# One core, attention and two feed-forward stages: a new order by hand of the attention work, with three pairs of groups under way at first

## The chip, the cores and the metric

The kernel runs on one core of a Trainium2 chip. The metric is the time of one execution on the device, in microseconds. The kernel before took 896.36 us (median of 2 runs, 894.23 to 898.49).

## The reference, cut to what matters

```python
def _attn_ref(q, k, v):                       # 4 batches, 8 heads, 576 positions, 64 wide, float32
    scores = 1.0 / np.sqrt(D) * np.matmul(q, k.transpose(0, 1, 3, 2))
    mask = (rel >= 0) & (rel < 64)            # each position sees itself and the 63 before it
    scores = np.where(mask, scores, -1000000000.0)
    attn = np.exp(scores - np.max(scores, axis=-1, keepdims=True))
    attn = attn / (np.sum(attn, axis=-1, keepdims=True) + 1e-09)
    return np.matmul(attn, v)
# heads side by side: x is 2304 x 512
h = (x @ w1) * (x @ w2) @ w3                  # 512 -> 1024 -> 1024
x = h @ w_out                                 # 1024 -> 512
h = x @ w_in                                  # 512 -> 2048
out = np.maximum(0.01 * h, h) @ w_out2        # 2048 -> 512
```

The weights arrive as 64-bit floats, which the kernel turns into 32-bit ones with bit operations.

## The kernel before

**Two phases.** In the first, three batches of four, every engine runs in an order that is written out by hand: each instruction is tied to the one before it on its engine (class `Strict`, L62). This phase holds the attention of all four batches, the conversion of weights, and `x @ w1` times `x @ w2` of batches 0 to 2. In the second (batch 3, the product of `w3` and `w_out`, and the two layers behind it), a scheduler sets the order.

**Steps.** The order of the first phase comes from numbered steps. `slot` (L509) does one: PE's attention events of this step, then one `ab` group (12 matmuls of 288 columns for `x @ w1` or `x @ w2`, L542), then the eviction of the group of the step before, then all other events of this step by rank, the small ranks first. `plan` (L467) and the table `PAIRS` (L461) say in which step each event stands. The first `HEAD` = 15 steps have no `ab` group. Each of batches 0 to 2 has 32 steps with one.

**A pair of groups.** A group `(m, hh, gr)` is three blocks of 64 queries for two heads, `m` = 2 x batch + quad of heads, `hh` the half of the quad, `gr` = 0 to 2. A pair is both halves. If its step is t, PE does `scores` in t (24 matmuls, which the trace shows as 48) and VectorE the six `maxima`; ScalarE the exponentials (`exps`) in t + 1 and t + 2, one half in each; `normal` (L221: sum plus 1e-9 on POOL, reciprocal on VectorE, multiplication on POOL) in t + 2 and t + 3; PE turns `s` (`turn`, `mm<-ident,s`) in t + 3 and t + 4, and it is copied out (`turned`); `av` and `av_out` stand in t + 4 and t + 5. `av_out` casts the result for `x` (ScalarE) and subtracts the cast from it (VectorE), as each 32-bit operand is split in a high and a low part. `prep` (L172) transposes `q` and `k` of the next quad on VectorE, six calls for each. The `pa` accumulator is one tile, whose halves take turns.

**Conversions.** `advance` (L323) moves a pipeline of units of 512 columns on by one: ScalarE scales the unit (`f`), and for `w1` and `w2` takes its low bits (`low_bits`, L318, into one buffer `low`); VectorE shifts and joins bits, one unit behind; and `store` (L280) casts the finished unit for `w` on ScalarE, and POOL (`w1`, `w2`) or VectorE (`w_out`) computes the low part `w<-f,w`. `f` has four buffers. Loads are issued by SP when a unit's bits are done.

**Products.** `b_out` (L560) multiplies the two `ab` groups on VectorE. Every eighth step (every fourth in parts of batch 0) two sums on POOL follow, `t3` and `p32`, as part of the eviction, ahead of the step's other events. Their stores `pb<-t` and `pb<-p` are put three steps later on SP. `t3` has one buffer.

## Time and profile before

| | us |
|---|---|
| median of 2 runs | 896.36 (894.23 to 898.49) |
| the profiled execution | 894.67 |
| its span, first to last instruction | 892.5 |
| TensorE matmul (PE) busy | 814.0 (91%) |
| VectorE (DVE) busy | 606.8 (68%) |
| ScalarE (ACT) busy | 459.6 (51%) |
| GpSimd (POOL) busy | 99.4 (11%) |

The profile is of one execution. PE is TensorE's matmuls, PEld its weight loads, SP the engine that issues transfers. The granted clock is the share of full speed that TensorE was allowed. Nearly all instructions go through one helper, so their line is L78 (ordered phase) or L76 (scheduled phase) and they are told apart by the names of tiles: `mm` scores and turns, `pa` the `av` accumulator, `ab`, `pr` and `o` the accumulators of the layers. In a row, `out<-in` names what is written and read, `x48` is the number of instructions in it, and a bracket says how long the engine had been idle and what released it.

### The profile page before, as it was taken

To read this page: it belongs to the slowest core of one execution; us is meant where nothing else is said; L and a number is where in the kernel's file an instruction comes from. 1 tells how busy PE (TensorE), PEld (TensorE's weight loads), DVE (VectorE), ACT (ScalarE), POOL (GpSimd) and SP (SyncE) were. 2 spreads that over 40 slices of the span, in tenths; PEclk is the share of its full clock that TensorE was granted. 3 is DMA by queue.
4 is the path that set the end of the run, shared out by engine and by line. 5 is a ranking of instruction groups with operands and counts; after the bars stand their busy time and mean duration, and the time that the engine had idled before them with its cause. 6 is when DMAs were issued, how large, how long until landed. Compare 5 with 4: busy or idle time off the path is not lost.

```text
span 892.5 us, 18232 instructions
## 1 busy us (share of the span) xinstructions
PE 814.0 (91%) x6856; PEld 777.2 (87%) x6856; DVE 606.8 (68%) x1446; ACT 459.6 (51%) x1103; POOL 99.4 (11%) x149
## 2 busy tenths in 40 slices
PE   3566869989897899999999999999999999999998
PEld 2355759988797889889999999999999999999998
DVE  5446453566355728688577888687775999897966
ACT  2445434444254443353455656565555886666644
POOL 2234242322222221000000000000000000000000
PEclk9667889999899999999999999999999999999999
DMA  9328534467343627655267745699899864443422
GB/s 275 120 81 203 191 106 137 125 171 216 129 101 96 175 68 225 214 163 164 77 195 213 222 145 168 213 305 349 303 320 294 281 210 158 119 149 110 142 72 71
DMA packets 121544, 157.96 MB, mean 177 GB/s; under 512 B 42736, under 2 KB 82928, under 8 KB 121456
## 3 DMA queue, kind: packets, MB, share of 16 engines
q1 hardware_dynamic: 121312, 156.66, 56.8%
q8 instruction: 54, 0.88, 0.4%
q14 instruction: 34, 0.28, 0.1%
q10 hardware_dynamic: 144, 0.13, 0.0%
HBM read 104.07 MB, written 52.69 MB: 176 GB/s over the span
## 4 chain that ended last, share of the span: by engine, by line
PE 71%; DVE 9%; ACT 5%; DMA 5%; POOL 4%; issue 4%; SPq 1%; POOLq 0%; DVEq 0%; ACTq 0%
PE pr L76 29%; PE o L76 20%; PE ab L78 10%; PE mm L78 6%; DVE f L78 3%; PE ab L76 2%; PE mm L76 2%; DMA wd<-f 2%; PE pa L78 2%; DMA pb<-t 2%; POOL s L78 2%; ACT s L78 1%; DVE f L76 1%; POOL w L78 1%; DVE qT L78 1%
## 5 line engine op out<-in xcount | busy, mean ns | idle before, releaser
L78 PE MATMUL ab<-x,w 128*128 128x288 f32 x1152 | 179.1, 311 | 0.0
L78 PEld LDWEIGHTS ab<-x,w 128*128 128x128 f32 x1152 | 164.4, 199 | 5.5 <-issue 3.6
L76 PE MATMUL pr<-yop,w 128*128 128x384 f32 x900 | 161.0, 337 | 0.5 <-ACT c L76 0.5
L76 PEld LDWEIGHTS pr<-yop,w 128*128 128x128 f32 x900 | 157.5, 188 | 1.3 <-ACT c L76 1.2
L76 PE MATMUL o<-yop,yop 128*128 128x256 f32 x777 | 94.9, 282 | 0.0
L76 PEld LDWEIGHTS o<-yop,yop 128*128 128x128 f32 x777 | 93.6, 189 | 0.0
L76 ACT COPY c<-pr 128x384 f32<-128x384 f32 x95 | 45.2, 479 | 63.3 <-PE pr L76 55.5
L78 PE MATMUL mm<-ident,s 128*128 128x128 f32 x144 | 30.6, 331 | 51.1 <-POOL s L78 46.9
L76 ACT CAST yop<-raw 128x256 fp32r<-128x256 f32 (+2 forms) x116 | 54.3, 491 | 37.2 <-PE o L76 33.8
L78 PEld LDWEIGHTS mm<-ident,s 128*128 128x128 f32 x144 | 19.2, 164 | 58.2 <-POOL s L78 57.1
L76 DVE TENSOR_TENSOR yop<-raw,yop 128x256 fp32r<-128x256 f32 (+2 forms) x116 | 58.0, 524 | 16.9 <-ACT yop L76 16.5
L78 ACT ACTIVATE s<-s,nm 128x128 f32<-128x128 f32 x144 | 56.1, 393 | 17.9 <-DVE nm L78 17.8
L76 ACT CAST yop<-f 128x512 fp32r<-128x512 f32 (+2 forms) x102 | 54.9, 567 | 18.6 <-DVE f L76 15.8
L76 DVE TENSOR_TENSOR yop<-f,yop 128x512 fp32r<-128x512 f32 (+2 forms) x102 | 59.3, 617 | 3.5 <-ACT yop L76 3.5
L76 DVE TENSOR_TENSOR c<-pr,c 128x384 f32<-128x384 f32 x74 | 40.7, 552 | 27.8 <-PE pr L76 13.7
L76 PEld LDWEIGHTS ab<-x,w 128*128 128x128 f32 x384 | 53.3, 188 | 1.8
L76 PE MATMUL ab<-x,w 128*128 128x288 f32 x384 | 54.8, 295 | 0.0
L76 PE MATMUL mm<-wf,w3T 128*128 128x512 f32 x192 | 51.0, 401 | 0.4 <-ACT w3T L76 0.4
L78 DVE TENSOR_TENSOR x<-pa,x 128x192 fp32r<-128x192 f32 x48 | 17.0, 354 | 46.4 <-ACT x L78 46.2
L78 DVE TENSOR_TENSOR p<-ab,io 128x288 f32<-128x288 f32 x48 | 21.7, 453 | 38.2 <-ACT s L78 13.4
L78 ACT COPY io<-ab 128x288 f32<-128x288 f32 x48 | 19.1, 397 | 54.2 <-PE ab L78 53.2
L78 DVE CUSTOM_DVE_ANT_0 s<-mm,mask 128x128 f32<-128x128 f32 x144 | 32.3, 287 | 20.2 <-PE mm L78 20.2
(121 smaller groups left out, 1438.0 us busy)
## 6 DMA issues: line engine op xcount, KB each, us to landing
hd<-c SPq DMA_DIRECT2D x96, 192.0 KB, 4.1
raw<-hd SPq DMA_DIRECT2D x32, 512.0 KB, 3.8
raw<-in_moe_w_dram SPq DMA_DIRECT2D x28, 512.0 KB, 4.6
raw<-in_moe_w_out_dram SPq DMA_DIRECT2D x24, 512.0 KB, 5.0
pb<-p SPq DMA_DIRECT2D x32, 288.0 KB, 4.6
raw<-in_moe_w_in_dram SPq DMA_DIRECT2D x16, 512.0 KB, 4.3
wd<-f SPq DMA_DIRECT2D x32, 256.0 KB, 4.6
raw<-wd SPq DMA_DIRECT2D x30, 256.0 KB, 4.6
```

The lines of the kernel that those rows point to most:

```text
L76: return f(*a, **k)
L78: r = f(*a, **k)
```

## The change

- `HEAD` is 13, and the pairs of batch 0 stand two steps apart instead of three (`PAIRS`); the pairs of batches 1 to 3 stand one to two steps earlier against the batch's first step.
- In batch 0 the scores stand ahead of the turns of their step. In batches 1 to 3 both halves' exponentials stand in t + 1, both divisions in t + 2 (the second behind the conversions of that step, rank 6.5), both turns in t + 4.
- In all batches both `av` stand in t + 5, with a new `pa` tile for each pair; the cast of the result is `x_hi` in t + 5, the subtraction `x_lo` in t + 6.
- `low` has two buffers, in turn; `pts` has two instead of three.
- The low part `w<-f,w` of a unit stands one step behind its cast, rank 1.
- The sums `t3` and `p32` stand at the end of their step (rank 8).
- Six transposes of the second quad stand in steps 0 and 1 instead of 0 to 2; `q` and `k` of the third quad are loaded in step 3 instead of 14, into other buffers; at the end of batch 2 the last conversions stand ahead of the last events.

```diff
@@ -58,7 +58,7 @@
-    HEAD = 15
+    HEAD = 13
@@ -150,7 +150,7 @@
     def loads_qk(m):
         b, quad = divmod(m, 2)
-        raw_qk[m] = [spare_tile("wf")[:, 0:EQ * D] if b else xb.tile([P, 2, S], F32, name="x", tag="x").rearrange("p s c -> p (s c)")
+        raw_qk[m] = [spare_tile("wf")[:, 0:EQ * D] if m > 2 else xb.tile([P, 2, S], F32, name="x", tag="x").rearrange("p s c -> p (s c)")
@@ -233,7 +233,7 @@
     def turned(g):
-        pts = att.tile([P, GT, P], F32, name="pts", bufs=3)
+        pts = att.tile([P, GT, P], F32, name="pts", bufs=2)
         (act.copy if g[0] > 1 else dve.tensor_copy)(pts, grp[g])
         grp[g] = pts
 
@@ -242,11 +242,9 @@
         b, quad = divmod(m, 2)
         vt = vts[2 * m + hh]
         pts = grp[g]
-        if not pa:
-            t = ps_at.tile([P, 4, P], F32, name="pa", tag="pa").rearrange("p t k -> p (t k)")
-            pa.extend(t[:, 2 * P * i:2 * P * i + GT * W] for i in range(2))
-        pa.append(pa.pop(0))
-        o = grp[g] = pa[-1]
+        if hh == 0:
+            pa[:] = [ps_at.tile([P, 4, P], F32, name="pa", tag="pa").rearrange("p t k -> p (t k)")]
+        o = grp[g] = pa[0][:, 2 * P * hh:2 * P * hh + GT * W]
         for t in range(GT):
             l = GT * gr + t
             a, n = (0, max(l - 1, 0) // 2) if (l % 2 or l == 0) else (1, (l - 2) // 2)
@@ -255,16 +253,19 @@
                 pe.matmul(o[W * h:W * h + W, W * t:W * t + W], lhsT=vt[:, (a + h) % 2, n + h * (4 + a), :],
                           rhs=pts[:, t, W * c:W * c + W], start=True, stop=True)
 
-    def av_out(g):
+    def xcols(g):
         m, hh, gr = g
         b, hp = m // 2, 2 * (m % 2) + hh
-        o = grp.pop(g)
         if (b, hp) not in xt:
             xt[b, hp] = xtile(b)
-        x = xt[b, hp]
-        cols = slice(gr * GT * W, (gr + 1) * GT * W)
-        act.copy(x[:, 0, cols], o)
-        dve.tensor_tensor(out=x[:, 1, cols], in0=o, in1=f32(x[:, 0, cols]), op=ALU.subtract)
+        return (xt[b, hp][:, i, gr * GT * W:(gr + 1) * GT * W] for i in range(2))
+
+    def x_hi(g):
+        act.copy(next(xcols(g)), grp[g])
+
+    def x_lo(g):
+        hi, lo = xcols(g)
+        dve.tensor_tensor(out=lo, in0=grp.pop(g), in1=f32(hi), op=ALU.subtract)
 
 
     def wslot(key):
@@ -284,14 +285,20 @@
                 slots[key] = wslot(key)
             t, sl = slots[key], slice(UC * half, UC * half + UC)
             act.copy(t[:, 0, sl], f)
-            (pool if key[0] in ("w1", "w2") else dve).tensor_tensor(out=t[:, 1, sl], in0=f, in1=f32(t[:, 0, sl]),
-                                                                     op=ALU.subtract)
+            later(1, lambda: (pool if key[0] in ("w1", "w2") else dve).tensor_tensor(
+                out=t[:, 1, sl], in0=f, in1=f32(t[:, 0, sl]), op=ALU.subtract), 1)
         return fin
+
+    def later(d, f, rank=8):
+        if Strict.on:
+            at(clock["t"] + d, rank, f)
+        else:
+            f()
 
...
@@ -316,7 +323,8 @@
         return t.rearrange("p k m -> p (k m)") if len(t.shape) == 3 else t
 
     def low_bits(u):
-        u["low"] = stage.tile([P, UC], I32, name="low", tag="low", bufs=1)
+        n_of["low"] += Strict.on
+        u["low"] = (att if n_of["low"] % 2 else stage).tile([P, UC], I32, name="low", tag="low", bufs=1)
         act.activation(out=u["low"], in_=flat(u["raw"]).bitcast(U8).rearrange("p (m e) -> p m e", e=8)[:, :, 3],
                        func=AF.Copy, scale=1.0 / 32, bias=-31.0 / 64)
 
@@ -458,8 +466,8 @@
     ev = {"pe": {}, "post": {}}
     clock = {"t": 0, "evict": None}
     START = [HEAD + 4 * KF * b for b in range(B)]
-    PAIRS = [[3 * i for i in range(2 * NG)]] + [[START[b] + t for t in ts]
-                                                for b, ts in enumerate(((6, 10, 15, 19, 24, 28), (1, 6, 11, 17, 22, 27), (0, 5, 11, 16, 21, 26)))]
+    PAIRS = [[0, 2, 4, 6, 8, 10]] + [[START[b] + t for t in ts]
+                                                for b, ts in enumerate(((4, 8, 13, 18, 23, 28), (1, 6, 11, 17, 22, 27), (0, 5, 10, 15, 20, 25)))]
 
     def at(t, rank, f, *a, pe=False):
         ev["pe" if pe else "post"].setdefault(t, []).append((rank, f, a))
@@ -472,39 +480,37 @@
             if b == 0:
                 order = [(quad, gr) for gr in range(NG) for quad in range(2)]
             for (m, gr), t in zip(order, PAIRS[b]):
-                at(t, 3, scores, m, gr, pe=True)
+                at(t, 3 if b else 0, scores, m, gr, pe=True)
                 for hh in range(2):
                     g = (m, hh, gr)
                     at(t, 3, maxima, g)
-                    at(t + 1 + hh, 4, exps, g)
-                    at(t + 2 + hh, 0, normal, g)
-                    at(t + 3 + hh, 1, turn, g, pe=True)
-                    at(t + 3 + hh, 1, turned, g)
-                    at(t + 4 + hh, 2, av, g, pe=True)
-                    at(t + 4 + hh, 2, av_out, g)
-                    done[2 * m + hh] = t + 4 + hh
+                    at(t + 1 + (0 if b else hh), 4, exps, g)
+                    at(t + 2 + (0 if b else hh), (0, 6.5)[hh] if b else 0, normal, g)
+                    at(t + (4 if b else 3 + hh), 1, turn, g, pe=True)
+                    at(t + (4 if b else 3 + hh), 1, turned, g)
+                    at(t + 5, 2, av, g, pe=True)
+                    at(t + 5, 2, x_hi, g)
+                    at(t + 6, 1, x_lo, g)
+                    done[2 * m + hh] = t + 5
                 if gr == 0:
                     for i in range(2 * EP):
                         if m == 1:
-                            at(i // 2, 2 if i < 2 else 5, prep, m, i)
+                            at(i // 3, 2 if i < 2 else 5, prep, m, i)
                         elif m:
                             at(t - 3 + i // 2, 5, prep, m, i)
                     if 2 <= m < 2 * B - 2:
                         at(t + 1, 7, lambda m: load(loads_qk(m)), m + 2)
-        for m, t in ((2, 14), (3, 21)):
+        for m, t in ((2, 3), (3, HEAD + 4)):
             at(t, 7, lambda m: load(loads_qk(m)), m)
         for n in range(NHP, B * NHP):
             at({4: 16, 5: done[0] + 1, 6: done[1] + 1}.get(n, done[n - 3] + 1), 7, lambda n: load(loads_v(n)), n)
-        for t in list(range(1, HEAD, 2)) + list(range(HEAD, HEAD + 4)) + list(range(HEAD + 4, HEAD + 22, 2)):
+        for t in [1, 3, 5, 7, 9, 10, 11, 13, 14, 15, 16, 17, 19, 21, 23, 25, 27, 29, 31]:
             at(t, 6, advance, PHASE_B)
         for b, stop in ((1, WO_FROM), (2, W3_FROM)):
             for i, t in enumerate(PAIRS[b + 1]):
                 for d in (0, 2, 4) if i % NG < 2 else (0, 4):
                     if t + d < START[b] + 4 * KF:
                         at(t + d, 6, advance, stop)
...
@@ -566,20 +572,18 @@
         if c and hf:
             p1, p2 = (prods.pop((p, i)) for i in range(2))
             t3 = gp.tile([P, NH], F32, name="t3", tag="t3", bufs=1)
-            sums = pool if Strict.on else dve
-            sums.tensor_tensor(out=t3, in0=p2[:, 1], in1=p2[:, 0], op=ALU.subtract)
-            sums.tensor_tensor(out=p2[:, 0], in0=p2[:, 0], in1=p1[:, 0], op=ALU.subtract)
+
+            def sums():
+                e = pool if Strict.on else dve
+                e.tensor_tensor(out=t3, in0=p2[:, 1], in1=p2[:, 0], op=ALU.subtract)
+                e.tensor_tensor(out=p2[:, 0], in0=p2[:, 0], in1=p1[:, 0], op=ALU.subtract)
+
+            later(0, sums)
             later(3, lambda: sp.dma_start(pb[b][:, 2:4, p], p2))
             later(3, lambda: sp.dma_start(pb[b][:, 4, p], t3))
         elif c:
             p1 = prods[p, hf]
             later(1, lambda: sp.dma_start(pb[b][:, 0:2, p], p1))
-
...
@@ -867,11 +871,11 @@
                             y_half(n, hh)
         if b == B - 2:
             clock["evict"]()
+            until(W3_FROM, W3_FROM)
             while ev["post"]:
                 for _, f, a in ev["post"].pop(min(ev["post"])):
                     f(*a)
             assert not ev["pe"]
-            until(W3_FROM, W3_FROM)
             Strict.on = False
```

On PE, from its first matmul on (`kT,qT` and `x` are the scores of the first and second quad, `ident,s` a turn, `pa` an `av`), the order before was:

```order
L78 MATMUL mm<-kT,qT 64x128 x24
L78 MATMUL mm<-ident,s 128x128 x3
L78 MATMUL mm<-x 64x128 x24
L78 MATMUL mm<-ident,s 128x128 x3
L78 MATMUL pa<-pts,vt 64x64 x12
L78 MATMUL mm<-ident,s 128x128 x3
L78 MATMUL mm<-kT,qT 64x128 x24
L78 MATMUL mm<-ident,s 128x128 x3
```

And now, in the same place:

```order
L78 MATMUL mm<-kT,qT 64x128 x24
L78 MATMUL mm<-x 64x128 x24
L78 MATMUL mm<-ident,s 128x128 x3
L78 MATMUL mm<-kT,qT 64x128 x24
L78 MATMUL mm<-ident,s 128x128 x6
L78 MATMUL pa<-pts,vt 64x64 x12
L78 MATMUL mm<-x 64x128 x24
L78 MATMUL mm<-ident,s 128x128 x6
L78 MATMUL pa<-pts,wf 64x64 x12
```

The third scores now stand ahead of the second turn, and from there on one pair's scores, two turns (of two different pairs) and two `av` repeat.

On POOL, in batch 0 around the first sums (`w` low parts, `rs` and `s` the two halves of a division, `t3` and `p32` the sums), the order before was:

```order
L78 TENSOR_TENSOR w_102<-f_836,w_102 128x512
L78 TENSOR_TENSOR t3_1140<-p32_1071 128x288
L78 TENSOR_TENSOR p32_1071<-p32_1071,p32_739 128x288
L78 TENSOR_SCALAR rs_1143<-sm_1121 128x3
L78 TENSOR_TENSOR s_1078<-s_1078,rs_1143 128x384
L78 TENSOR_TENSOR w_103<-f_925,w_103 128x512
L78 TENSOR_SCALAR rs_1179<-sm_1147 128x3
L78 TENSOR_TENSOR s_1083<-s_1083,rs_1179 128x384
L78 TENSOR_TENSOR w_103<-f_984,w_103 128x512
L78 TENSOR_TENSOR t3_1298<-p32_1209 128x288
```

And now:

```order
L78 TENSOR_TENSOR t3_1166<-p32_1107 128x288
L78 TENSOR_TENSOR p32_1107<-p32_1107,p32_787 128x288
L78 TENSOR_TENSOR w_103<-f_950,w_103 128x512
L78 TENSOR_SCALAR rs_1295<-sm_1268 128x3
L78 TENSOR_TENSOR s_1240<-s_1240,rs_1295 128x384
L78 TENSOR_TENSOR w_103<-f_1043,w_103 128x512
L78 TENSOR_SCALAR rs_1303<-sm_1272 128x3
L78 TENSOR_TENSOR s_1245<-s_1245,rs_1303 128x384
L78 TENSOR_TENSOR t3_1324<-p32_1264 128x288
L78 TENSOR_TENSOR p32_1264<-p32_1264,p32_944 128x288
```

The two sums stood directly ahead of a division of the same step; now they stand in step 25, three steps ahead of the next division (step 28), and the second sums, of step 29, behind both halves of it.

On PE in batch 1, five steps with one pair were, before:

```order
L78 MATMUL ab<-x,w 128x288 x36
L78 MATMUL mm<-ident,s 128x128 x3
L78 MATMUL ab<-x,w 128x288 x12
L78 MATMUL mm<-ident,s 128x128 x3
L78 MATMUL pa<-pts,vt 64x64 x6
L78 MATMUL ab<-x,w 128x288 x12
L78 MATMUL pa<-pts,vt 64x64 x6
L78 MATMUL mm<-kT,qT 64x128 x24
```

And now:

```order
L78 MATMUL mm<-kT,qT 64x128 x24
L78 MATMUL ab<-x,w 128x288 x48
L78 MATMUL mm<-ident,s 128x128 x6
L78 MATMUL ab<-x,w 128x288 x12
L78 MATMUL pa<-pts,vt 64x64 x12
```

Four `ab` groups stand between scores and the first turn instead of three, four as before up to the second turn, and each kind of attention work is in one piece.

## Rows read from the trace of the kernel before

**Rows 1.** The profile's page: its first line.

```profile
span 892.5 us, 18232 instructions
```

**Rows 2.** Busy us (and instructions) of each engine by stretch, granted clock, transfers.

```profile
9.20:62.97 53.77, 29.03 (x412) 22.99 (x412) 27.11 (x104) 24.84 (x87) 15.90 (x24) 0.73 0.53 147
62.97:88.93 25.96, 18.44 (x133) 16.35 (x130) 16.82 (x40) 13.21 (x34) 9.04 (x9) 0.76 0.72 177
88.93:170.38 81.45, 69.64 (x792) 63.44 (x793) 37.19 (x132) 35.87 (x124) 29.25 (x39) 0.90 0.42 128
170.38:334.69 164.31, 146.06 (x1693) 134.95 (x1693) 86.35 (x300) 74.36 (x251) 39.09 (x62) 0.96 0.50 142
```

**Rows 3.** Waits (us, times, longest): PE 0–62.97, PE 62.97–334.69, ACT 0–90.

```profile
PE mm L78 <- POOL s L78: 13.8, 5, 4.7
...
PE mm L78 <- POOL s L78: 33.0, 14, 4.9
PE mm L78 <- DVE qT L78: 4.2, 2, 2.4
...
ACT low L78 <- DVE f L78: 26.2, 8, 7.2
```

**Rows 4.** PE in order of time: start us, us, what, idle before.

```profile
9.21 2.84 PE L78 MATMUL mm<-kT,qT 32*64 32x128 f32 x48 [9.21 <-DVE qT L78]
...
25.26 0.90 PE L78 MATMUL mm<-ident,s 128*128 128x128 f32 x3 [1.63 <-POOL s L78]
...
31.41 0.57 PE L78 MATMUL pa<-pts,wf 128*64 128x64 f32 x12 [0.81 <-DVE x L78]
...
62.97 2.64 PE L78 MATMUL ab<-x,w 128*128 128x288 f32 x12
...
88.93 1.98 PE L78 MATMUL mm<-kT,qT 32*64 32x128 f32 x48 [2.36 <-DVE qT L78]
```

**Rows 5.** Groups by shape, 0 to 90: busy us, mean ns, idle before.

```profile
L78 ACT ACTIVATE s<-s,nm 128x128 f32<-128x128 f32 x36 | 14.0, 393 | 10.5 <-DVE nm L78 10.5
...
L78 POOL TENSOR_TENSOR w<-f,w 128x512 fp32r<-128x512 f32 x9 | 11.4, 1272 | 36.4 <-ACT w L78 36.4
L78 POOL TENSOR_TENSOR s<-s,rs 128x384 f32<-128x384 f32 x12 | 10.5, 872 | 5.1 <-DVE rs L78 4.4 <-PE mm L78 0.7
...
L78 DVE SCALAR_TENSOR_TENSOR f<-f,low 128x512 int32<-128x512 int32 x11 | 8.1, 736 | 0.0
L78 DVE CUSTOM_DVE_ANT_0 s<-mm,mask 128x128 f32<-128x128 f32 x36 | 8.1, 286 | 10.3 <-PE mm L78 10.3
...
L78 ACT CAST w<-f 128x512 fp32r<-128x512 f32 x9 | 5.4, 603 | 0.0
L78 ACT ACTIVATE low<-raw 128x512 int32<-128x512 uint8 x8 | 5.4, 669 | 21.1 <-DVE f L78 21.1
L78 DVE STREAM_TRANSPOSE x<-x 128x384 f32<-128x384 f32 x6 | 4.7, 876 | 0.0
```

**Rows 6.** The chain that ended last, ahead of the wait at 133.

```profile
123.42 4.54 DMA pb<-t
...
128.09 0.82 POOL t L78
...
128.98 1.25 POOL p L78
```

**Rows 7.** POOL and DVE in order of time, around 24.4.

```profile
24.39 0.82 POOL L78 TENSOR_TENSOR s<-s,rs 128x384 f32<-128x384 f32 x1 [0.29 <-DVE rs L78]
...
24.46 1.29 DVE L78 SCALAR_TENSOR_TENSOR f<-wf,f 128x512 int32<-128x512 int32 x1
```

**Rows 8.** PE in order of time: scores of steps 48 and 53, batch 3's first.

```profile
170.38 1.14 PE L78 MATMUL mm<-kT,qT 32*64 32x128 f32 x48
...
181.44 1.14 PE L78 MATMUL mm<-kT,qT 32*64 32x128 f32 x48
...
334.69 4.91 PE L76 MATMUL ab<-x,w 128*128 128x288 f32 x36
```

9 lines of the change are left out of this document (1 added, 8 removed).

## The prediction

> **What bounds the kernel now.** I read the page's span first, then the busy time by stretch, then PE's waits in the two parts of the ordered phase, then the engines in order of time around the longest waits. The span is 892.5 [rows 1]. PE is the engine that the rest serves: after 334.69, where batch 3 begins, it hardly stops, and there the order changes in a few rows only. Before it, PE is busy 29.0 of 53.8 us up to the first `ab` group at 62.97, 18.4 of 26.0 up to 88.93, 69.6 of 81.5 up to 170.38 and 146.1 of 164.3 up to 334.69, at a mean granted clock of 0.73, 0.76, 0.90 and 0.96 [rows 2]. So what can be won lies ahead of 334.69, as idle time and as work done at the lower of TensorE's two levels (1.2 and 2.4 GHz).
>
> The waits name one place: PE's turn of `s` waits for POOL's multiplication, 13.8 us before 62.97 and 33.0 us in 14 waits after it; besides, 4.2 us for `qT` [rows 3]. POOL is not busy then: it stands behind something. I followed each of the 14 in order of time; of the 33.0 us, six waits (19.3 us) have the sums `t3` and `p32` ahead of the division's `rs`; the clearest is at 133, where the sum waited 4.5 us for the store of the `t3` before it [rows 6]. Five (11.0 us) have the cast's low part `w` ahead, which waits for ACT, whose `low` waits for VectorE to be done with the one `low` buffer: 26.2 us in 8 waits [rows 3]. Three (2.8 us) have neither.
>
> A step (below) is one call of the function that orders the work, with one `ab` group from step 15 on. Undisturbed, five steps with one pair of groups take 181.44 - 170.38 = 11.06 us, 2.21 a step [rows 8]. The pairs number the steps: 88.93 is step 21, 170.38 step 48, 334.69 step 111. Steps 21 to 47 took 81.5 us instead of 59.7, steps 48 to 110 took 164.3 instead of 139.2: 46.9 us lost, of which 30.1 is idle [rows 2] and the rest slower matmuls.
>
> **The change part by part.** *The head, to the first `ab`.* The start stays: scores at 9.21 for 2.84 us [rows 4], six maxima (6 x 0.29), four transposes of the next heads (4 x 0.78) [rows 5], so the second scores start at 16.8. Then, behind them, a turn (0.90 [rows 4]), and the third scores start at 20.5. From there a pair costs PE 2.84 for scores, 2 x 0.90 for turns and 2 x 0.57 for `av` [rows 4], 5.8 us as long as PE runs as it did here, and nothing need stand between: a pair's turns come behind the next pair's scores, so its division has another pair's work to hide behind. For the other engines a pair is less: ACT 6 x 0.39 for exponentials, 0.67 each for scale and `low` and 0.60 for the cast, 4.3; POOL 2 x 0.87 + 1.27 = 3.0 and its small adds; VectorE 1.7 for maxima and 1.5 for two bit operations, and its copies [rows 5]. So a pair lies between 4.6 (PE at its high level, ACT with its hand-overs the longest) and 5.8; I take 5.6, as the clock stood at 0.73 in the old head. Three pairs on, the last scores start at 37.3. From the last scores to the first `ab` runs one chain: scores 2.8, turn 0.9 and copy, maxima, exponentials 1.2, division 0.7, a `w` ahead of the last one 1.3, multiplication 0.9, turn 0.9, two `av` 1.2: about 11. The first `ab` is at **48.3** (45.3 to 48.9), 14.7 us sooner.
>
> *Steps 13 to 16.* A conversion in each of four steps. Its cast (0.60), POOL's low part (1.27), which frees a buffer, the scale and `low` (0.67 each) run in a ring: 3.2 us each, longer than PE's step. VectorE has six transposes in the same steps. I take **12.1** (10 if the ring starts ahead, 15.2 if each round is held 0.6 longer, as a bit operation at 24.46 was [rows 5, 7]). Scores of batch 1 then start at 60.4 with four `ab` behind them; before it was 88.93 with six.
>
> *The rest of the ordered phase* is now 92 steps (17 to 108). At 2.21 that is **203.3**. Both turns stand in one step, a step later for the first; the sums stand behind the divisions; the low parts a step later. So the eleven waits with sums or casts ahead (30.3 us) go. The `t3` store still has one buffer: the sums of step 29 wait for the store issued in step 28, some 4.5 us, but the next division on POOL is in step 33, so it lies beside PE's `ab`. What is late next are VectorE's transposes. I leave the 2.8 and the 4.2 us, and as much again for the clock after them and for small waits of the second turn, whose step is not later than before: **12** in all (4 to 46.9, all of the old loss).
>
> *Costs at nothing.* The third `pts` buffer goes: a pair's copy now waits for the `av` two behind it, which is done a turn earlier. Loads on SP keep their order but for a few that move by a step or two; values for the next groups have four steps, 8.8 us, against the store's 4.5. One accumulator for both halves: the next `av` comes two steps on in the head and five later, and the subtraction needs one. In the head the subtraction, ahead of a copy, hides under PE's scores; without that cover it is no more than 0.74 a half, what a bit operation on more columns takes [rows 5].
>
> *The sum.* 48.3 + 12.1 + 203.3 + 12 = 275.7 where batch 3 starts, against 334.69: 59 us. The rest stays 892.5 - 334.7 = 557.8, so the span is 833.5, and with the 2.2 us that lay outside the span (894.67 - 892.5) 835.7. The profiled run was 1.7 below the median of the runs shown, so on that scale **837**.
>
> One row speaks against it. At 24.46 a bit operation on VectorE took 1.29 us beside POOL's multiplication of 24.39, where its kind takes 0.74 in the mean [rows 5, 7]. The change brings more of both at once. The Trainium skill, in "SBUF — State Buffer", section "Who interferes with whom", says that a VectorE instruction with two SBUF inputs and a GpSimd one that reads SBUF exclude each other, the second being blocked. By that, the trace agrees at this place; it is the second rival.
>
> **The rivals.** *The waits stay in other dress.* For: the second division's reciprocal stands behind a conversion on VectorE, and one `t3` buffer remains. Against: that reciprocal stood behind the same three operations before, and only three waits had neither sum nor cast ahead. If half of the old 46.9 stays, and the head takes 6.4 a pair, it is 50.7 + 15.2 + 203.3 + 23.5 = 292.7, so **854**; with three quarters, 866.
>
> *VectorE and POOL exclude each other.* Each pair meets two bit operations and two multiplications; at 0.6 us each on both, a head pair takes up to 6.4 and each of the four steps 3.8. That is 50.7 + 15.2 + 203.3 + 16, so **847**. Against: beyond step 17 PE's 2.2 us a step cover it.
>
> *Only the head wins.* The 14.7 us come, and the rest keeps its whole loss on 92 steps: 48.3 + 15.2 + 203.3 + 46.9, batch 3 at 313.7, **875**. Against it: the rows of POOL show the causes of most waits, and they go.
>
> *Slower.* The twelve sums of batches 0 to 2 hold POOL until the `t3` store has landed; moved behind the divisions they stand ahead of the next pair's and of the low parts. That costs more than the 59 us won once PE loses 4.9 us at each of the twelve, as much as its longest single wait for POOL now, 4.9 [rows 3]. If PE bears all of it, landing 4.5 and two sums 0.8 and 1.25 [rows 6], 6.6 each, it is **916**. Against: the next division is two to five steps behind, 4.4 to 11 us.
>
> That the change does not do what it says I rule out from the order on PE and POOL.
>
> **How the numbers follow.** Forecast 0.62 (824 with the first `ab` at 45.3, the ring at 10 and 4 left; 843 with 18 left), exclusion 0.13 (843 to 850), waits in other dress 0.17 (850 to 868), only the head 0.05 (870 to 885), slower 0.03. The range 822 to 866 leaves out under 2 in 10. A measurement of this kernel tells about 2% from no change, which is 878.4 and 914.3 here: faster 0.94, within 2% 0.04, slower 0.02.
>
> **What will show it.** First `ab` within 45 to 51; a pair every 5 to 6 us before it, counted by its scores; batch 1's scores at 58 to 64; batch 3 at 265 to 285; PE's waits for POOL after the first `ab` under 10 us instead of 33.0; no sum between a division and the one before it in the same step; ACT's `low` hardly waiting. It is wrong if pairs of the head come at 7 us or more (POOL or VectorE is the bound), if PE's `av` waits for the subtraction of the pair before, or if batch 3 itself, whose order is the same, grows from 557.8 because its conversions come too late.

## The result and the profile after

The changed kernel took **834.5 us** (median of 2 runs, 833.16 to 835.85) against 896.36: a ratio of 0.931, with a 95% interval of 0.9195 to 0.9425. It is 61.9 us faster. 837 was predicted, with a range of 822 to 866.

The profiled execution took 833.16 us. The first line of its page stands against [rows 1]:

```profile
span 831.4 us, 18254 instructions
```

The stretches that answer to [rows 2], with the same columns: up to the first `ab`, steps 13 to 16, the rest of batch 0 with the first pairs of batch 1, and up to batch 3.

```profile
8.91:47.84 38.93, 25.59 (x441) 20.43 (x441) 31.00 (x121) 26.23 (x98) 18.73 (x28) 0.87 0.73 203
47.84:61.66 13.82, 9.72 (x78) 9.25 (x76) 12.00 (x20) 8.50 (x18) 4.26 (x4) 0.86 0.53 128
61.66:131.26 69.60, 65.63 (x816) 61.66 (x817) 40.34 (x136) 37.77 (x128) 32.44 (x41) 0.98 0.66 195
131.26:271.60 140.34, 135.27 (x1697) 128.91 (x1693) 88.16 (x300) 72.57 (x251) 41.56 (x62) 1.00 0.58 164
```

The first `ab` comes at 47.84 instead of 62.97, and batch 3 starts at 271.60 instead of 334.69: 63.1 us sooner, which is the whole gain. What follows batch 3's start takes 559.8 us against 557.8. In the last stretch PE is busy for 135 of 140 us at a granted clock of 1.00.

PE's waits, to be read beside [rows 3]: the first two rows are up to 47.84, the last three from 47.84 to 271.60.

```profile
PE mm L78 <- POOL s L78: 5.3, 4, 2.4
...
PE mm L78 <- DVE pts L78: 2.6, 1, 2.6
...
PE mm L78 <- POOL s L78: 7.4, 9, 1.3
PE mm L78 <- DVE qT L78: 4.8, 2, 4.1
PE pa L78 <- DMA vt<-in_v_dram: 0.8, 1, 0.8
```

Behind the first `ab` the waits for POOL fell from 33.0 us to 7.4, and the longest from 4.9 to 1.3. The longest wait that is left there is for one of VectorE's transposes, 4.1.

PE in order of time, beside [rows 4]: second and third scores, two later ones, the turns of the tail, the first `ab`, and batch 1's first scores.

```profile
16.28 2.84 PE L78 MATMUL mm<-x 32*64 32x128 f32 x48 [4.53 <-DVE rs L78]
...
19.88 2.12 PE L78 MATMUL mm<-kT,qT 32*64 32x128 f32 x48
...
29.32 1.54 PE L78 MATMUL mm<-kT,qT 32*64 32x128 f32 x48
...
34.39 2.65 PE L78 MATMUL mm<-x 32*64 32x128 f32 x48
...
42.05 0.90 PE L78 MATMUL mm<-ident,s 128*128 128x128 f32 x3 [2.44 <-POOL s L78]
...
45.53 0.90 PE L78 MATMUL mm<-ident,s 128*128 128x128 f32 x3 [2.59 <-DVE pts L78]
...
47.84 3.25 PE L78 MATMUL ab<-x,w 128*128 128x288 f32 x12
...
61.66 1.76 PE L78 MATMUL mm<-kT,qT 32*64 32x128 f32 x48 [4.09 <-DVE qT L78]
```

From 19.88 to 34.39 three pairs took 14.5 us, 4.84 each. Scores that took 2.84 at the start took 2.12 and 1.54 there. The granted clock is 1.00 up to 34.39, 0.55 in the last scores (2.65 again) and 0.50, the lower of TensorE's two levels (1.2 GHz), from 42.05 to the first `ab`; in the kernel before it is 0.50 in each of the last four scores of the head, which took 2.83 to 2.84. The granted clock doesn't tell it all: the first two scores took 2.84 at 1.00, in both kernels. From the last scores to the first `ab` it is 13.4 us, with two waits of 2.4 and 2.6.

The tail on VectorE and POOL in order of time, beside [rows 7], shows what those two waits stand behind:

```profile
39.64 0.69 DVE L78 SCALAR_TENSOR_TENSOR f<-wf,f 128x512 int32<-128x512 int32 x1
...
40.25 0.68 DVE L78 SCALAR_TENSOR_TENSOR f<-f,low 128x512 int32<-128x512 int32 x1
...
40.85 0.17 DVE L78 RECIPROCAL rs<-rs 128x3 f32<-128x3 f32 x1
...
41.17 0.83 POOL L78 TENSOR_TENSOR s<-s,rs 128x384 f32<-128x384 f32 x1 [1.47 <-DVE rs L78]
41.38 1.16 DVE L78 SCALAR_TENSOR_TENSOR f<-raw,f 128x512 int32<-128x512 int32 x1
...
41.95 1.71 POOL L78 TENSOR_TENSOR w<-f,w 128x512 fp32r<-128x512 f32 x1
...
42.46 1.75 DVE L78 SCALAR_TENSOR_TENSOR f<-f,low 128x512 int32<-128x512 int32 x1
```

POOL had its part of the division (`rs`) done, but the reciprocal stood behind two bit operations, so the multiplication began at 41.17 and the turn at 42.05. Then bit operations and POOL's work stretched each other: bit operations took 1.16 and then 1.75 instead of 0.68, POOL's `w` 1.71 instead of 1.27. The next division stands behind both, and the turn of 45.53 behind it.

An undisturbed pair of batch 2 (scores of steps 67 and 72), beside [rows 8]:

```profile
178.43 1.14 PE L78 MATMUL mm<-kT,qT 32*64 32x128 f32 x48
...
189.14 1.12 PE L78 MATMUL mm<-kT,qT 32*64 32x128 f32 x47
```

Five steps take 10.71 us, where [rows 8] had 11.06.

### The profile page after: what moved, and what is told of

Its sections match the earlier page's. It is cut to its first block, busy times and chain, and to the rows that moved or that the text cites. A ratio compares the mean times of both kernels' runs of the same rounds, so it can differ in the third digit from the quotient of the medians.

```text
span 831.4 us, 18254 instructions
## 1 busy us (share of the span) xinstructions
PE 788.5 (95%) x6856; PEld 761.0 (92%) x6856; DVE 611.8 (74%) x1446; ACT 456.7 (55%) x1103; POOL 101.3 (12%) x149
## 4 chain that ended last, share of the span: by engine, by line
PE 72%; DVE 11%; DMA 9%; issue 3%; POOL 2%; ACT 2%; SPq 0%; DVEq 0%; ACTq 0%; POOLq 0%
PE pr L76 28%; PE o L76 22%; PE ab L78 12%; PE mm L78 5%; DMA wd<-f 4%; DVE f L76 2%; PE pa L78 2%; DMA raw<-in_moe_w_dram 2%; PE ab L76 2%; DVE f L78 2%; POOL s L78 1%; PE mm L76 1%; DVE s L78 1%; DMA vt<-in_v_dram 1%; DVE x L78 1%
## 5 line engine op out<-in xcount | busy, mean ns | idle before, releaser
L78 PE MATMUL ab<-x,w 128*128 128x288 f32 x1152 | 165.7, 301 | 0.0
L78 PEld LDWEIGHTS ab<-x,w 128*128 128x128 f32 x1152 | 156.5, 191 | 3.6 <-issue 3.2
L76 ACT CAST yop<-f 128x512 fp32r<-128x512 f32 (+2 forms) x102 | 54.9, 567 | 20.1 <-DVE f L76 15.3
L76 PEld LDWEIGHTS ab<-x,w 128*128 128x128 f32 x384 | 53.5, 189 | 1.8
L76 PE MATMUL ab<-x,w 128*128 128x288 f32 x384 | 55.1, 296 | 0.0
L76 ACT ACTIVATE f<-raw 128x512 f32<-128x512 f32 x40 | 26.6, 674 | 35.4 <-DMA wd<-f 28.0
L76 PE MATMUL o<-w,yop 128*128 128x256 f32 x378 | 45.9, 282 | 0.0
L78 POOL TENSOR_TENSOR s<-s,rs 128x384 f32<-128x384 f32 x48 | 41.2, 858 | 36.2 <-DVE rs L78 34.3
```

What stands on the lines that cost most here:

```text
L76: return f(*a, **k)
L78: r = f(*a, **k)
```

## The experiments

All on one core. Each kernel whose name begins with u_ is the changed kernel with one edit undone; b_ is the kernel before with one part of the change (and the new order of the last conversions of batch 2). "First `ab`" and "batch 3" are the starts of the first `ab` matmuls of the run and of batch 3 in the profile, "rest" is the span behind the latter.

| kernel | median us | first ab | batch 3 | rest |
|---|---|---|---|---|
| before | 896.36 | 63.0 | 334.7 | 557.8 |
| after | 834.50 | 47.8 | 271.6 | 559.8 |
| u_low | 834.65 | 47.8 | 271.3 | 561.2 |
| u_head | 836.92 | 50.1 | 274.9 | 560.2 |
| u_xlo | 839.13 | 49.9 | 275.1 | 562.4 |
| u_sums | 844.15 | 47.3 | 281.1 | 561.1 |
| u_turn | 845.28 | 48.0 | 282.4 | 560.6 |
| u_cast | 849.71 | 55.1 | 289.7 | 559.0 |
| u_sct | 872.99 | 55.7 | 313.2 | 561.6 |
| b_cast | 876.52 | 54.9 | 315.7 | 559.3 |
| b_sums | 883.24 | 62.9 | 321.6 | 557.9 |
| x_fill | 830.42 | 46.6 | 268.8 | 559.7 |
| c1 | 832.01 | 47.6 | 269.3 | 559.0 |
| c2 | 831.55 | 46.4 | 268.0 | 559.6 |

The rest differs by up to 3.4 us between the kernels that stem from the one after, whose order there is the same, so one profile's stage is good to about that much, and the parts ahead of batch 3 are compared by their starts. The kernel before, timed again beside these runs, had medians of 894.14 to 896.51, so medians compare to some 2 us; where less is at stake, the ratios to it are given.

### Pairs three steps apart again (u_head)

```diff
-    HEAD = 13
+    HEAD = 16
-    PAIRS = [[0, 2, 4, 6, 8, 10]] + ...
+    PAIRS = [[0, 3, 6, 9, 12, 15]] + ...
-        for t in [1, 3, 5, 7, 9, 10, 11, 13, 14, 15, 16, 17, 19, ...]:
+        for t in [1, 3, 5, 7, 9, 11, 13, 15, 16, 17, 18, 19, 20, 22, ...]:
```

> The kernel after with batch 0's pairs three steps apart again and a head of 16 steps (15 don't leave room for the subtraction that now stands a step later); the conversions' steps are shifted with it. Theory 1, that the spacing of the pairs is what brings the first ab sooner: first ab at 58 to 64 instead of 47.8, a pair every 8 us or more, 10 to 16 us slower in all. Theory 2, that in the head the order within a step (scores ahead of the turns, conversions' low parts a step later, two low buffers) does it and empty steps cost nothing: first ab at 47 to 51, 0 to 3 us slower.

Measured: 836.92 (834.74 to 837.94), ratio 0.9333 (0.9314 to 0.9352), which can hardly be told from u_low's 0.9315 (0.9295 to 0.9335); first `ab` at 50.1. The second theory holds. PE in order of time in u_head, from the fourth scores on:

```profile
30.20 1.54 PE L78 MATMUL mm<-x 32*64 32x128 f32 x48
...
45.30 1.54 PE L78 MATMUL mm<-x 32*64 32x128 f32 x48
...
50.10 2.11 PE L78 MATMUL ab<-x,w 128*128 128x288 f32 x10
```

Pairs did come more slowly, every 7.2 us ((45.30 - 9.24) / 5, the first scores being at 9.24). But from the last scores to the first `ab` it is 4.8 us instead of 13.4, since the last pair's turns and `av` now stand among `ab` groups. Three pairs under way at first are not what the head's gain is made of: what a wider spacing loses between the pairs, it gives back behind the last one.

### The subtraction directly behind its cast (u_xlo)

```diff
-                    at(t + 6, 1, x_lo, g)
+                    at(t + 5, 2, x_lo, g)
```

> The kernel after with one edit undone: the subtraction for x stands directly behind its cast again, a half at a time, in the step of the av, instead of a step later. In the kernel before, PE's second av waited for that subtraction (7.4 us in 4 waits in a run of it with the sums moved), and three steps between the pairs turned out to cost 2.4 us only. Theory 1, that this pair of waits, ACT's cast behind a late low and VectorE's subtraction behind the cast, is what the old head was made of: first ab at 52 to 58 instead of 47.8, 5 to 12 us slower in all. Theory 2, that one accumulator for both halves, with both av in one step, is what removes the wait, so that the subtraction's place is free: first ab within 1 us of 47.8, all in all within 2 us.

Measured: 839.13 (838.16 to 841.34), ratio 0.9392 (0.9356 to 0.9428); first `ab` at 49.9, batch 3 at 275.1. It lies between the theories: 2 us in the head, 1.4 behind it, and the remainder in the rest, which this edit doesn't touch. No `av` of the head waits for the subtraction; its turns wait for POOL's `s`, 8.6 us in 5 waits instead of 5.3 in 4. In the kernel before, up to 62.97, four did:

```profile
PE pa L78 <- DVE x L78: 6.9, 4, 3.2
```

So these `av` waits must have gone by another edit (the one accumulator is the likely one). What the later step saves fits the time in which a subtraction that waits for its cast holds VectorE's queue: behind the first `ab` it is 26.2 us in 34 waits here and 0.9 in one in the kernel after.

### One low buffer again (u_low)

```diff
-        u["low"] = (att if n_of["low"] % 2 else stage).tile([P, UC], I32, name="low", tag="low", bufs=1)
+        u["low"] = stage.tile([P, UC], I32, name="low", tag="low", bufs=1)
```

> The kernel after with one buffer for the low bits again. Theory 1, that ACT's wait for that buffer (26.2 us in 8 waits before) was part of the chain ahead of PE: 5 to 15 us slower than the kernel after, most of it before batch 1's first scores (first ab at 50 or later, batch 1's scores at 66 or later), ACT's low waiting for VectorE's f 10 us or more. Theory 2, that ACT's wait was hidden, since ACT is not the bound: within 3 us of the kernel after, though ACT waits as long.

Measured: 834.65 (833.67 to 836.21), the same as the kernel after at every stage. The second theory holds for the time, but not for its reason: with one buffer ACT's `low` waited only 4.7 us in 6 waits up to 62. So another buffer is not what ended the 26.2 us of [rows 3]; that VectorE ran late in the old order is the likely cause, and was not tried. Its four runs also stand for the kernel after, which was run twice.

### Sums ahead of the divisions again (u_sums)

```diff
-            later(0, sums)
+            sums()
```

> The kernel after with one edit undone: the two sums t3 and p32 stand with the eviction again, ahead of the step's divisions. My prediction put six waits (19.3 us of the kernel before) on the sums. Theory 1, that the new table of pairs already keeps sums and divisions apart (sums in steps 25, 29, 37, 45, 53 and so on, divisions elsewhere but for a few steps): 2 to 6 us slower than the kernel after, all of it behind the start of batch 1, first ab unchanged at 47.8. Theory 2, that the place within the step is what removed those waits: 15 to 25 us slower, PE's waits for s from POOL back at 20 us or more.

Measured: 844.15 (842.1 to 846.63), 9.7 slower than the kernel after, all behind the first `ab`: between the theories. PE's waits for `s` there are 13.8 us instead of 7.4. Most of what they grew by is at one place, step 69, where sums and a division coincide (the turn that waits for it is in step 71). POOL and PE in u_sums in order of time (`t` is `t3`, `p` `p32`):

```profile
188.51 0.79 POOL L78 TENSOR_TENSOR t<-p 128x288 f32<-128x288 f32 x1 [13.07 <-DMA pb<-t]
189.38 0.79 POOL L78 TENSOR_TENSOR p<-p,p 128x288 f32<-128x288 f32 x1
190.25 0.23 POOL L78 TENSOR_SCALAR rs<-sm 128x3 f32<-128x3 f32 x1
...
190.84 0.83 POOL L78 TENSOR_TENSOR s<-s,rs 128x384 f32<-128x384 f32 x1 [0.36 <-DVE rs L78]
...
191.72 0.90 PE L78 MATMUL mm<-ident,s 128*128 128x128 f32 x3 [3.96 <-POOL s L78]
...
193.77 3.23 PE L78 MATMUL ab<-x,w 128*128 128x288 f32 x12
```

The store of `t3`, issued by SP at 181.74, held the sum until 188.5, the sum held the division, and the division PE for 3.96 and 0.59 us. Behind that, 12 `ab` matmuls took 3.23 us instead of the 1.83 that they take in the undisturbed pair at 186.54 of the kernel after: the granted clock, 1.00 there, is 0.50 here from the end of the wait to 198.40. The pair took 18.3 us (180.07 to 198.40) instead of 10.7: 4.6 idle and 3.0 slower matmuls, 7.6 of the 9.7. In the kernel after the same place reads:

```profile
185.25 0.83 POOL L78 TENSOR_TENSOR s<-s,rs 128x384 f32<-128x384 f32 x1 [0.36 <-DVE rs L78]
186.29 0.81 POOL L78 TENSOR_TENSOR t<-p 128x288 f32<-128x288 f32 x1 [0.21 <-DMA pb<-t]
```

Both halves' divisions are through before the sum asks for the buffer.

### Exponentials, divisions and turns in the old steps (u_turn)

```diff
-                    at(t + 1 + (0 if b else hh), 4, exps, g)
-                    at(t + 2 + (0 if b else hh), (0, 6.5)[hh] if b else 0, normal, g)
-                    at(t + (4 if b else 3 + hh), 1, turn, g, pe=True)
...
+                    at(t + 1 + hh, 4, exps, g)
+                    at(t + 2 + hh, 0, normal, g)
+                    at(t + 3 + hh, 1, turn, g, pe=True)
...
```

> The kernel after with the exponentials, divisions and turns of batches 1 to 3 in the old steps: first half a step ahead of the second, turns in t + 3 and t + 4, av still together in t + 5. Theory 1, that the later turn of the first half is what took POOL's division off PE's path: 5 to 12 us slower than the kernel after, all behind 61.7, as waits of PE for s. Theory 2, that with sums and low parts out of the way the old steps had time enough: within 2 us, waits for s under 10 us as in the kernel after.

Measured: 845.28 (844.76 to 846.4), 10.8 slower, all behind the first `ab`. The first theory holds. The waits for `s` behind 62 are 11.6 us with a longest of 4.1, at the same pair again, which takes 17.6 us:

```profile
187.94 0.79 POOL L78 TENSOR_TENSOR t<-p 128x288 f32<-128x288 f32 x1 [3.06 <-DMA pb<-t]
...
190.27 0.83 POOL L78 TENSOR_TENSOR s<-s,rs 128x384 f32<-128x384 f32 x1 [0.36 <-DVE rs L78]
...
191.16 0.90 PE L78 MATMUL mm<-ident,s 128*128 128x128 f32 x3 [4.09 <-POOL s L78]
```

The sums stand behind the first half's division here, but the second half's is a step later and so stands behind the sums. At this pair the sums at the end of the step help only if both halves divide in one step: here the two edits are halves of one. (Elsewhere the sums' new place helps without it, as b_sums shows below.) Besides, undisturbed pairs of steps 46 and 77 take 11.02 and 11.03 us here, against 10.71 and 10.69 in the kernel after.

### Low parts in the step of their cast (u_cast)

```diff
-            later(1, lambda: (pool if key[0] in ("w1", "w2") else dve).tensor_tensor(
-                out=t[:, 1, sl], in0=f, in1=f32(t[:, 0, sl]), op=ALU.subtract), 1)
+            (pool if key[0] in ("w1", "w2") else dve).tensor_tensor(out=t[:, 1, sl], in0=f, ...)
```

> The kernel after with the low part of a unit (w<-f,w on POOL) in the step of its cast again. My prediction put five waits (11.0 us) on that low part standing ahead of a division and waiting for ACT. Theory 1, that the step between them is what took this away: 3 to 12 us slower than the kernel after, some of it in the head (first ab at 49 to 53), PE's waits for s up by as much. Theory 2, that two buffers for the low bits alone remove ACT's lateness, so that POOL finds the cast done: within 2 us.

Measured: 849.71 (848.38 to 851.94), 15.2 slower, the most of any single part. That is more than either theory had. First `ab` at 55.1: 7.3 us of it in the head, where the first theory had 1 to 5. POOL and PE in u_cast, near the end of the head:

```profile
49.97 1.26 POOL L78 TENSOR_TENSOR w<-f,w 128x512 fp32r<-128x512 f32 x1 [1.43 <-ACT w L78]
51.31 0.23 POOL L78 TENSOR_SCALAR rs<-sm 128x3 f32<-128x3 f32 x1
...
51.90 0.83 POOL L78 TENSOR_TENSOR s<-s,rs 128x384 f32<-128x384 f32 x1 [0.36 <-DVE rs L78]
...
52.78 0.90 PE L78 MATMUL mm<-ident,s 128*128 128x128 f32 x3 [3.28 <-POOL s L78]
```

POOL stood with the low part in front and waited 1.43 us for ACT's cast; the division and PE's turn behind it waited too, the turn 3.28 us.

### The three together (u_sct)

The last three edits undone at once.

> The kernel after with three edits undone at once: the sums ahead of the divisions, the low parts in the step of the cast, exponentials, divisions and turns of batches 1 to 3 in the old steps. Undone one by one they cost 9.5, 15 and 11 us. Theory 1, that they take away different waits: 31 to 39 us slower than the kernel after (866 to 874). Theory 2, that each covers for the other, so that one alone undone hides part of its price: more than 42 us slower (over 877). Theory 3, that they remove the same waits: under 25 us slower (below 860).

Measured: 872.99 (868.54 to 876.59), 38.5 slower than the kernel after; one by one they cost 9.7 + 10.8 + 15.2 = 35.7. The total lies where the first theory had it, but not because each edit has waits of its own. From the scores of step 67 to those of step 72 it is 9.1 us longer than in the kernel after (19.84 against 10.71), where u_sums and u_turn alone cost 7.6 and 6.9: these two take away the same wait. From step 26 to 31 and from 82 to 87 it is 18.16 and 17.58 against 12.03 and 11.80, where no edit alone costs more than 0.9: these waits come back only when several are undone. That overlap and extra loss nearly offset each other is luck. PE's waits for POOL's `s` behind the first `ab` are back:

```profile
PE mm L78 <- POOL s L78: 28.8, 11, 6.5
```

### One part alone on the kernel before (b_sums, b_cast)

The same edits, added to the kernel before: the sums at the end of their step, or the low part a step behind its cast. Both kernels also have the last conversions ahead of batch 2's last events, as the change has it; what that is worth alone was not run.

> The kernel before with one part of the change alone: the sums t3 and p32 at the end of their step instead of ahead of its divisions (and, as the change has it, the last conversions ahead of batch 2's last events). Theory 1, by my reading of six waits (19.3 us): 15 to 25 us faster than the kernel before, PE's waits for s behind 62.97 down from 33.0 to about 14, the head as before. Theory 2, that the sums only move the wait to the next user of POOL (low parts, then the next division) while the store of t3 is out: 0 to 8 us faster.

> The kernel before with one part of the change alone: the low part of a unit (w<-f,w) a step behind its cast (and the last conversions ahead of batch 2's last events). Undone from the kernel after, this part cost 15 us, 7 of them in the head. Theory 1, that POOL's wait for ACT's cast is a cause by itself: 10 to 20 us faster than the kernel before, first ab at 55 to 60 instead of 63. Theory 2, that it counts only in the new head, where nothing else holds PE, and that with one low buffer and the old av the same waits come back in other dress: 0 to 6 us faster, first ab at 61 or later.

Measured: b_sums 883.24 (881.78 to 884.39), 12.7 us below the kernel before on the same chip (895.9), b_cast 876.52 (872.34 to 877.5), 17.6 below (894.14). The ratios are 0.987 (0.9848 to 0.9893) and 0.9797 (0.9761 to 0.9833). The sums lie between their theories, the low part within the first. Waits behind the first `ab` of b_sums and of b_cast, where [rows 3] has 33.0 in 14:

```profile
PE mm L78 <- POOL s L78: 24.3, 14, 4.1
...
PE mm L78 <- POOL s L78: 21.8, 12, 4.2
```

In step order, the six waits that the prediction put down to sums (steps 28, 33, 56, 72, 88 and 104) fall from 19.3 to 6.8 us in b_sums and to 16.5 in b_cast; the five put down to low parts (steps 18, 19, 24, 25 and 29) fall from 11.0 to 3.0 in b_cast. But in b_sums 5.1 us come back a step later, at the turn of the second half (steps 29, 57 and 73), ahead of whose division the sums now stand, as its second theory had it. Steps 28 and 29 in b_sums, where they took 3.02 and 1.78 before:

```profile
112.00 0.55 PE L78 MATMUL mm<-ident,s 128*128 128x128 f32 x3 [1.62 <-POOL s L78]
...
118.21 0.55 PE L78 MATMUL mm<-ident,s 128*128 128x128 f32 x3 [4.06 <-POOL s L78]
```

Alone the low part brings the first `ab` from 63.0 to 54.9, with one low buffer and the old `av` (whose waits for the subtraction stay, 7.9 us in 4). Its price is nearly the same from both ends (17.6 added, 15.2 undone), and so is that of the sums (12.7, 9.7).

### POOL's low part as a fill (x_fill)

The low parts of `w1` and `w2` are left zero: the same place on POOL, without an operand to read, and so without a wait for the cast.

```diff
-            later(1, lambda: (pool if key[0] in ("w1", "w2") else dve).tensor_tensor(
-                out=t[:, 1, sl], in0=f, in1=f32(t[:, 0, sl]), op=ALU.subtract), 1)
+            if key[0] in ("w1", "w2"):
+                later(1, lambda: pool.memset(f32(t[:, 1, sl]), 0.0), 1)
+            else:
+                later(1, lambda: dve.tensor_tensor(out=t[:, 1, sl], in0=f, ...), 1)
```

> The kernel after, but POOL fills the low parts of w1 and w2 with zeros instead of computing them (these low parts are left out of the result): the same instruction in the same place, one that reads nothing from SBUF. Theory 1, that VectorE's bit operations and POOL's two-input operations hold each other (bit operations of 1.0 to 1.75 us beside POOL's work against 0.7 alone, w of 1.7 against 1.27): bit operations beside the fill take 0.8 or less, the first ab comes 1 to 3 us sooner and batch 1's scores 2 to 4 us sooner than 47.8 and 61.7. Theory 2, that these long instructions lie beside PE's work or behind other waits: first ab and batch 1's scores within 1 us.

Measured: 830.42 (829.88 to 833.97), ratio 0.9292 (0.9262 to 0.9323), which overlaps u_low's; first `ab` 1.2 sooner, batch 1's first scores at 58.27, 3.4 sooner, batch 3 2.8 sooner. By these starts the first theory holds, in its lower half for the head. VectorE, POOL and PE in x_fill: the places that answer to 41.38, 42.46 and 61.66 above, and between them two bit operations beside a row of fills:

```profile
41.19 1.16 DVE L78 SCALAR_TENSOR_TENSOR f<-raw,f 128x512 int32<-128x512 int32 x1
...
42.27 0.68 DVE L78 SCALAR_TENSOR_TENSOR f<-f,low 128x512 int32<-128x512 int32 x1
...
46.55 0.68 DVE L78 SCALAR_TENSOR_TENSOR f<-raw,f 128x512 int32<-128x512 int32 x1
46.55 2.38 POOL L78 MEMSET w<- 128x512 f32 x5
...
47.15 0.69 DVE L78 SCALAR_TENSOR_TENSOR f<-f,low 128x512 int32<-128x512 int32 x1
...
58.27 1.14 PE L78 MATMUL mm<-kT,qT 32*64 32x128 f32 x48 [2.55 <-DVE qT L78]
```

The one beside POOL's multiplication (which still reads SBUF) keeps its 1.16; the two beside the fills take 0.68 and 0.69. The one of 42.27, which took 1.75 beside the subtraction, takes 0.68, but starts as the fill of 41.74 (0.53) ends. The fill is also shorter than the subtraction (0.53 against 1.27) and waits for no cast: five of them run in a row at 46.55, ahead of their steps, so that POOL does nothing beside VectorE in steps 14 to 16. So the 2.8 us by which batch 3 starts sooner are an upper bound for what the two engines cost each other by `w`.

### Two candidates (c1, c2)

c1 puts the third quad's transposes a step earlier and the conversion of step 17 in step 30; c2 also moves a conversion from step 10 to step 4.

```diff
-                            at(t - 3 + i // 2, 5, prep, m, i)
+                            at(t - (4 if m == 2 else 3) + i // 2, 5, prep, m, i)
-        for t in [1, 3, 5, 7, 9, 10, 11, 13, 14, 15, 16, 17, 19, 21, 23, 25, 27, 29, 31]:
+        for t in [1, 3, 5, 7, 9, 10, 11, 13, 14, 15, 16, 19, 21, 23, 25, 27, 29, 30, 31]:   (c1)
+        for t in [1, 3, 4, 5, 7, 9, 11, 13, 14, 15, 16, 19, 21, 23, 25, 27, 29, 30, 31]:    (c2)
```

> A candidate: the kernel after with the transposes of the third quad of heads one step earlier (steps 13 to 15) and the conversion of step 17 moved to step 30. If the 4.1 us wait for qT at batch 1's first scores (61.7) and the 1.1 to 1.3 us waits for s behind step 17 are VectorE's and ACT's order, as the trace reads: batch 1's scores at 57 to 60, 3 to 6 us faster than the kernel after. If VectorE's sum of work in steps 13 to 16 is the bound (busy 12.0 of 13.8 us), the wait moves to another place and it is within 2 us.

> A candidate: the kernel after with the transposes of the third quad a step earlier, the conversion of step 17 moved to step 30 (both of which alone gave 832.0 us against 834.5), and two conversions of the head's end moved forward (steps 4 and 5 in place of 9 and 10's pair), so that the tail behind the last scores holds less work. If the tail's 2.4 to 2.6 us waits come from the bit operations of step 10's conversion ahead of the reciprocal: first ab at 45 to 46.5 instead of 47.6, 829 to 831 us. If the earlier conversions delay the pairs by as much: first ab at 47 to 49, 831 to 834 us.

Measured: c1 832.01 (830.1 to 833.15), c2 831.55 (829.42 to 832.45, 5 runs). In c1 batch 1's first scores come without a wait, 5.5 us sooner than in the kernel after:

```profile
56.14 1.14 PE L78 MATMUL mm<-kT,qT 32*64 32x128 f32 x48
...
61.51 3.96 PE L78 MATMUL ab<-x,w 128*128 128x288 f32 x28 [0.83 <-POOL w L78]
```

The four steps 13 to 16 then take 8.5 us (47.6 to 56.1), PE's own pace. More than half of the 5.5 is given back by new waits (for `w` here, later for a copy and for `qT`), and batch 3 starts 2.3 sooner. c2 brings the first `ab` to 46.4, in the range of its better case, and batch 3 3.6 sooner. Both are some 3 us below the kernel after: in c1 the scores come a little sooner than its first case had them, but the gain of 2.5 us lies short of that case's 3 to 6; c2's time lies in its worse case. Their ratios, 0.9296 (0.9274 to 0.9318) and 0.9299 (0.9273 to 0.9326), overlap with u_low's, which stands for the kernel after; that they are faster is likely, not settled.

## Why the prediction was right, and where its steps were not

| step | predicted | measured |
|---|---|---|
| third scores | 20.5 | 19.9 |
| a pair of the head | 5.6 (4.6 to 5.8) | 4.84 |
| last scores to first `ab` | 11 | 13.4 |
| first `ab` | 48.3 | 47.8 |
| steps 13 to 16 | 12.1 (10 to 15.2) | 13.8 |
| 92 steps | 203.3 + 12 | 209.9 |
| batch 3 | 275.7 | 271.6 |
| rest | 557.8 | 559.8 |
| profiled execution | 835.7 | 833.2 |

**The claim that carried it.** The loss lay ahead of batch 3, as waits for POOL behind sums and behind low parts of casts, and it would go. It went: 63.1 us ahead of batch 3, and 33.0 us of waits became 7.4. Sums and low parts were counted at 19.3 + 11.0 = 30.3 us of idle; alone on the kernel before they bring 12.7 + 17.6 = 30.3. **That the two totals agree is luck.** The places were read rightly: without the sums ahead, the sums' six waits fell by 12.4, and without the low parts ahead, the low parts' five by 8.0. What was wrong is what each edit brings alone. Of the sums' 12.4, 5.1 come back a step later as long as the halves divide in different steps. And 8.1 of the low part's 17.6 lie in the head, where none of its price had been booked.

**The head: right time, mostly another cause.** The sum ascribed 14.7 us to the new order of the pairs, closer together and with scores ahead of turns. u_head shows that the spacing is worth 2.3 us at the first `ab`; b_cast and u_cast show that 7 to 8 of the 15.1 are the low part's step, and u_xlo that 2.0 are the subtraction's. About 3 are left for what wasn't undone alone, scores ahead of turns and one accumulator among it. The prediction also left out a wait of the old head, 6.9 us of `av` for the subtraction, which is gone. Two terms were off and offset each other. The pair was taken near its slow bound because the old head's clock was 0.73; the granted clock was 1.00 over the three pairs, and a pair took 4.84, near the lower bound of 4.6. The tail was taken as one chain, with nothing of the conversions in it but one `w`; step 10's two bit operations stood ahead of a reciprocal, and step 11's ran against POOL.

**Steps 13 to 16: the wrong ring.** The term was made from ACT and POOL handing a unit on, 3.2 us a round (four rounds are 12.8, where the sum took 12.1). c1 keeps those four conversions, moves the transposes, and the four steps take 8.5: PE does not wait for the ring in these steps, and 1.1 us in the steps behind them. What held batch 1's scores at 61.66 were the six transposes, which the prediction named and didn't price, behind other work on VectorE, busy 12.0 of 13.8 us. Since c1 does the same six transposes and reaches the scores in 8.5, it is their place in VectorE's order and not the sum of its work. The term came out only 1.7 off because one queue's length happened to be near the other's.

**The pace.** 2.21 a step was read from [rows 8] and kept; undisturbed it became 2.14, 6.4 us on 92 steps. The turns of a pair and its `av` now stand in one piece each. u_turn splits the turns again: one undisturbed pair still takes 10.75 (108.78 to 119.53, the same steps as 109.76 to 120.51 in the kernel after), but others take 11.02 and 11.03 instead of 10.71 and 10.69. So at most pairs the split turns go with 0.3 us, nearly the whole 0.35; what `av` in one piece adds wasn't undone alone and stays open. At 2.14 the measured 209.9 leaves 12.8 for waits and slower matmuls, where 12 was left (the terms that the prediction names, 2.8 + 4.2 and as much again, are 14).

**Costs at nothing.** The third `pts` buffer, the one accumulator and the loads show no wait of PE above 0.8 us (`pa` for `vt`). A wait of ACT is new. Behind the first `ab` it stands twice for the load of a unit's raw weights, 2.8 us in step 16 (at 60.16) and 5.0 in step 17 (at 66.92):

```profile
ACT f L78 <- DMA raw<-in_moe_w_dram: 7.8, 2, 5.0
```

The kernel before has no such wait there. The division for which PE waits 1.27 us at 73.78 stands behind it in the chain that ended last, so it may cost PE a part of that. The prediction put ACT's lateness down to the one low buffer; u_low shows that the second is worth nothing here.

**The rivals.** VectorE and POOL do hold each other, but what POOL's low parts add to it is up to 2.8 us on the end, where the rival had 10 for low parts and multiplications: that the rest of the stretching lies beside PE's work fits this, and isn't shown. What the multiplications add wasn't taken away. The rule of the Trainium skill that was weighed ("SBUF — State Buffer", section "Who interferes with whom") says that such instructions exclude each other; the trace agrees, with the 1.16, 1.71 and 1.75 us above and x_fill's 0.68 and 0.69 beside fills. The slower case, the `t3` store, is a real mechanism and not a large one: it cost PE 4 us of idle at one step when u_sums or u_turn let a division stand behind it, and POOL 0.21 at that step in the kernel after. Waits in other dress remained at the 12.8 us named.

**What would show it** came as said, but for one: a pair every 4.8 us and not 5 to 6. Of what would show it wrong, one may be there in small: batch 3's part takes 559.0 to 562.4 us in all kernels that stem from the one after and 557.8 to 559.3 in the others. Why was not traced.

**What stays open.** Sums, low parts and turns undone together leave 23.4 us between u_sct and the kernel before by the medians (896.4 - 873.0), and 17.7 by the profiles: 7.3 ahead of the first `ab` and 14.2 between there and batch 3, less 3.8 that the rest is longer. What makes them (`av` in one piece, a last pair that is scored at 39 instead of 60 and so is mostly done before `ab` starts, the new table of steps) was not tried one by one. `av` in one piece can't be much of it: undisturbed pairs take 10.74 to 11.04 us in u_sct, against 11.06. And the table moves less than the list of the change says: the pairs of batch 2 and the last of batch 1 keep their steps.

## What to carry over

When an in-order engine of little load (POOL, busy 12%) is what TensorE waits for, look at what stands in front on its queue, and put an instruction that waits for another engine a step behind its producer: that one line, the low part a step later, was worth 15 to 18 us here, more than any rearrangement of TensorE's own order that was undone alone. Moving what stands in front pays only as far as the next user of the queue doesn't then wait behind it: of what the sums' move took away, 5.1 us came back a step later. Adding a part alone to the old kernel and undoing it alone from the new one gives its price from both ends; where parts are undone together, look at single waits, since a sum that comes out right can hide some that overlap and some that are new. In a hand-set order empty steps cost little, so a count of steps is no time: the head took nearly as long with 16 steps as with 13.

## What the runs showed of the hardware

- A bit operation on VectorE that starts during POOL's two-operand instruction ends 0.54 to 0.56 us after POOL's, whether it started 0.07 or 0.5 us into it: 41.38 + 1.16 against 41.17 + 0.83, 42.46 + 1.75 against 41.95 + 1.71, and in [rows 7] 24.46 + 1.29 against 24.39 + 0.82. It does nearly all of its 0.68 us behind POOL's end. It goes the other way round too: POOL's `w` at 41.95, started during a bit operation, took 1.71 instead of 1.27. Beside a fill, which reads nothing from SBUF, it takes 0.68 and 0.69 (x_fill).
- A wait costs more than its idle time. In u_sums 4.6 us of idle made one pair 7.6 us longer, as 12 `ab` matmuls behind it took 3.23 us instead of 1.83, at a granted clock of 0.50 instead of 1.00. The clock fell in the wait of 3.96 us and was back at 1.00 at 198.40. In the head of the kernel before it fell to 0.50 at about 24, in the second of two waits of 2.04 and 1.63 us, and it was 0.50 in all later scores there, which took 2.83 to 2.84; in the kernel after it was 1.00 until 34.39, with scores of 2.12 and 1.54.
